# Fused attention and sticky expert routing on one core: own buffers for the DMA-turned exponentials, pair and bias loads issued behind the transpositions, and new keys for the 16-bit products

## The chip, the cores and the metric

One core of one Trainium2 chip runs the whole program. The metric is the device time of one execution in microseconds (us); where several executions are told of, their median stands. The engines are TensorE (PE in the rows; its weight loads, which run beside it, are PEld), VectorE (DVE), ScalarE (ACT), GpSimd (POOL) and SyncE (SP), which here only issues DMAs.

## The reference, cut to what is computed

```
B, H, S, D = 4, 8, 576, 64
scores = q @ k.T / sqrt(D) + bias(|i - j|, i)     # bias: MLP 1 -> 32 -> 8 heads
attn = exp(scores - max);  attn /= attn.sum(-1) + 1e-09
x = (attn @ v), heads side by side                # (4, 576, 512), float32
logits, gate = x @ w_gate, sigmoid(x @ w_local)   # 8 experts
e = argmax(logits[s]) if s == 0 or gate[s] < 0.5 else e of the token before
out[s] = softmax(logits[s])[e] * (relu(x[s] @ w1[e]) @ w2[e])
```

The `bias` depends on the row and the distance only, so it is the same for all four batches. A wrong sign of `gate - 0.5` or a wrong argmax sends a token to another expert, so the scores and the products with the values are computed to about single precision, by pairs of 16-bit numbers (a high half and a low half) where they aren't computed in single precision.

## The kernel before

**Stages.** The bias tables are built first and written to device memory (`bias_d`). Then comes attention, then the routing of the tokens by the logits, then the expert blocks, whose weights stream in from 1 MB loads. The change touches attention alone.

**Pairs and units.** Attention goes through 16 pairs of a batch `b` and two neighbouring heads `p` (`pairs`). A pair has five query tiles in the order 1, 2, 0, 3, 4 (`QORD`), four of 128 rows and one of 64. A unit is one query tile and one head (`hh`); the tile of 64 rows is one unit for both heads, so a pair has 9 units and the program 144. `emit_s(u)` does a unit: TensorE multiplies queries and keys (L305, L306), VectorE adds the bias and takes the row maximum (L325), ScalarE takes the exponential `e` and its row sum (L330).

**Two ways to turn the exponentials.** The products with the values need the exponentials turned, with keys on the partitions. Mostly TensorE turns them (`emit_t`, L398) and ScalarE copies them out (L404). In nine of the pairs, `DMP`, called P0 to P8 here (batch and heads in the order in which the kernel goes through them: heads 1 for four batches, then four pairs of heads 2 and 3, and one more), the first two query tiles, 1 and 2, go another way. ScalarE copies `e` to a 16-bit high half (L336). `emit_lo` has VectorE subtract to get the low half (L346), and SyncE issues one DMA that turns both halves of that query tile at once (L350) into the tile `eT`. The first of the two transpositions of a pair is called T0, the second T1. Then `av_split` does 27 matmuls on 16-bit numbers (L363 and L369) with the pair's values, which `prefetch` splits into 16-bit halves `v16`. The remaining three query tiles go through TensorE and single precision (`emit_av`, L428).

**Buffers.** The turned 16-bit tile takes its place in the pool `et`, two buffers, where the single-precision turned tiles of the other query tiles live too. The pool `e16` for both halves ahead of the transposition has two, `v16` three. A pair's loads land in `qf` (two buffers) and two `kf` (three buffers for both), from which GpSimd casts and subtracts the 16-bit halves `qs`, `kh`, `kl` (four buffers): L122 is such a cast, L119 such a subtraction.

**What goes out.** When a pair is done, `emit_rows` scales its rows, ScalarE makes their 16-bit high halves (L482) and GpSimd the low halves, in the tile `xo` (one buffer). `store_rows` stores them by two DMAs (L492, L495), which for P0 to P8 stand in a list, `stores`, until `LST` units later.

**The order of work.** Steps are put in a list by a key, counted in units: `at(u + 0.1, unit_r, u)` comes 0.1 behind the scores of unit u. `unit_s` emits a unit, `unit_r` what is due of `stores` and `pend` (the query tiles that wait for `emit_lo`). `LA0` holds the keys of the three parts of `av_split`, counted from the last unit of the second query tile. The program is emitted in the order of the keys. From P0 to P8, SyncE runs exactly in that order; the order of the other engines is chosen by a scheduler when the kernel is built, from costs that it assumes.

**Loads.** `prefetch(gi)` is called with the first unit of a query tile. At the first tile of a pair it calls `load_pair` for the pair two further on: four DMAs on SyncE (L141 for `qf`, L143 twice for `kf`, L145 for the values `vt`). At the third tile it loads the next heads' bias tiles (`load_bias`, L166 to L168, three DMAs for one query tile, and L171).

Of the kernel before, what the change touches and what calls it, by code (L numbers as in the profile page):

```python
# [7 lines left out]
F32 = mybir.dt.float32  # L8
F16 = mybir.dt.float16
# [12 lines left out]
NQ = 5  # L22
NP = H // 2
# [5 lines left out]
QORD = (1, 2, 0, 3, 4)  # L29
# [20 lines left out]
def build(tc, nc, io):  # L50
# [20 lines left out]
    def pool(name, bufs, stack=None, **kw):  # L71
        return (stack or p1).enter_context(tc.tile_pool(name=name, bufs=bufs, **kw))
# [4 lines left out]
    et_p = pool("et", 2)  # L77
# [40 lines left out]
    def sub_pool(out, in0, in1):  # L118
        nc.gpsimd.tensor_tensor(out=out, in0=in0, in1=in1, op=ALU.subtract)  # L119
# [134 lines left out]
    pairs = [(p, b) for p in range(NP - 2) for b in range(B)]  # L254
# [7 lines left out]
    e_t, eT_t, hs_t = {}, {}, {}  # L262
    e16_t, v16_t, av_t = {}, {}, {}
    DMP = pairs[B:B + 9]
    dmx = ExitStack()
    dbox = {}
    pend, ucur = [], [0]
    stores, LST = [], 5

    def prefetch(gi):  # L270
        p, b, qt = groups[gi]
        if (p, b) in DMP and qt == QORD[0]:
            if "e" not in dbox:
                open_right()
            v16 = dbox["v"].tile([128, 2, NQ, 128], F16, name="v16")
            nc.vector.tensor_copy(out=v16[:, 0], in_=v_t[b, p])
            sub_pool(v16[:, 1], v_t[b, p], v16[:, 0])
            v16_t[p, b] = v16
        if p == 0:
            if G0 - 6 <= gi < G0 - 1:  # L280
                load_bias(1, QORD[gi - G0 + 6])
            if G0 - 6 <= gi < G0 - 4:
                load_pair(gi - (G0 - 6), 1, wr_t[KORD[-1]])
        else:
            if qt == QORD[0]:
                nx = gi // NQ + 2
                if nx < len(pairs):
                    load_pair(pairs[nx][1], pairs[nx][0])
            if p + 1 < NP and qt == QORD[2]:
                for x in (((0, 1), (2,), (3,), (4,)) if p < NP - 2 else ((0, 1, 2), (3, 4), (), ()))[b]:  # L290
                    load_bias(p + 1, QORD[x])

    def emit_s(u):
        gi, hh = units[u]
        p, b, qt = groups[gi]
        if hh != 1:
            prefetch(gi)
# [45 lines left out]
    def emit_lo(gi):  # L343
        p, b, qt = groups[gi]
        e, e16 = e_t.pop(gi), e16_t.pop(gi)
        nc.vector.tensor_tensor(out=e16[:, 1], in0=e, in1=e16[:, 0], op=ALU.subtract)  # L346
        if (p, b, 0) not in eT_t:
            eT_t[p, b, 0] = et_p.tile([128, 9, 320], F32, name="eT").rearrange("p k i -> p (k i)").bitcast(F16)
        eT = eT_t[p, b, 0][:, 0:18 * 256].rearrange("p (k i) -> p k i", i=256)
        nc.sync.dma_start(  # L350
            out=eT[:, :, QOFF[qt]:QOFF[qt] + 128], in_=e16.rearrange("p t j -> p (t j)"), transpose=True
        )

    def av_split(p, b, part=None):
        if part in (None, 0):
            av_t[p, b, 0] = av_ps.tile([128, 512], F32, name="av")
        av = av_t[p, b, 0]
        eT = eT_t[p, b, 0][:, 0:18 * 256].rearrange("p (t k i) -> p t k i", t=2, i=256)
        v16 = v16_t[p, b]
        terms = ((0, 0), (0, 1), (1, 0))  # L360
        if part in (None, 0):
            for n, (te, tv) in enumerate(terms):
                nc.tensor.matmul(out=av[:, 0:256], lhsT=v16[:, tv, 4], rhs=eT[:, te, 4], start=(n == 0), stop=False)  # L363
        for n, (te, tv) in enumerate(terms):
            if part not in (None, n):
                continue
            for j in range(4):
                for x in range(2):
                    nc.tensor.matmul(  # L369
                        out=av[64 * x:64 * x + 64, 0:256], lhsT=v16[:, tv, j, 64 * x:64 * x + 64],  # L370
                        rhs=eT[:, te, j + 5 * x], start=False, stop=(n == 2 and j == 3),
                    )
        if part not in (None, 2):
            return
        eT_t.pop((p, b, 0))
        v16_t.pop((p, b))
        if (p, b) == DMP[-1]:
            open_w()
        xt = xt_t[p, b] = xt_p.tile([128, SP], F32, name="xt")
        if p >= NP - 2:  # L380
            nc.vector.memset(xt[:, S:SP], 0.0)
        nc.vector.tensor_copy(out=xt[:, 0:256], in_=av[:, 0:256])
# [181 lines left out]
    def open_right():  # L564
        p0.close()
        rbox["x"] = ctx.enter_context(tc.tile_pool(name="x", bufs=2, side="right"))
        rbox["p"] = p2.enter_context(tc.tile_pool(name="rt", bufs=1, side="right"))
        dbox["e"] = dmx.enter_context(tc.tile_pool(name="e16", bufs=2, side="right"))
        dbox["v"] = dmx.enter_context(tc.tile_pool(name="v16", bufs=3, side="right"))
        nc.gpsimd.tensor_copy(out=iota16, in_=iota)  # L570
        nc.gpsimd.tensor_copy(out=ident16, in_=ident)
        nc.gpsimd.tensor_copy(out=amat16, in_=amat[:, 0:2])
# [65 lines left out]
    bias_step(12)  # L638
    LB0, LC0, LO0 = 3.2, 6, 1.28
    LTS = (3.2, 3.2, 2.95, 3.2, 3.95)  # L640
    LA0, LAN, LA1, LL, LOUT = (5.8, 8.55, 8.8), 10.62, (6.35, 6.6), 8.6, 8.72
    NU = len(units)
    ex_t = {}

# [396 lines left out]
            bias_step(BSTEP[s])  # L1041

    def unit_r(s):
        while stores and stores[0][0] <= s:
            store_rows(*stores.pop(0)[1:])
        while pend and pend[0][0] < s:
            emit_lo(pend.pop(0)[1])

    def unit_x(s):
        for st in steps:  # L1050
# [26 lines left out]
    def at(key, f, *a):  # L1077
        ev.append((key, len(ev), partial(f, *a)))

    for u in range(NU):  # L1080
        gi, hh = units[u]
        p, b, qt = groups[gi]
        at(u, unit_s, u)
        at(u + 0.1, unit_r, u)
        at(u + (LB0 if p == 0 else LTS[QORD.index(qt)]), emit_t, u)
        at(u + 0.4, unit_x, u)
        if qt == QORD[1] and hh == 1:
            if (p, b) in DMP:
                for n in range(3):
                    at(u + LA0[n], av_split, p, b, n)  # L1090
            elif p:
                at(u + LAN, emit_av, p, b, 0)
            else:
                at(u + LC0 + 0.6, emit_av, p, b, 0)
        if qt == 4:
            if p:
                if LA1[0] == LA1[1]:
                    at(u + LA1[0], pair_av1, p, b, None)
                else:
                    at(u + LA1[0], pair_av1, p, b, 0)  # L1100
                    at(u + LA1[1], pair_av1, p, b, 1)
                at(u + LL, pair_gates, p, b)
                at(u + LOUT, pair_out, (p, b, gi))
            else:
                at(u + LC0 + 0.6, pair_av1, p, b, None)
                at(u + LC0 + LO0 - 0.01, pair_gates, p, b)
                at(u + LC0 + LO0, pair_out, (p, b, gi))
# [70 lines left out]
    oa, at = rtile([128, NG2, NB], "oa", F16), rtile([128, NG2, NB], "at", F16)  # L1178
# [346 lines left out]
```

## Time and profile before

| | us |
|---|---|
| median of three executions (lowest, highest) | 581.92 (577.92, 582.97) |
| the profiled execution | 580.57 |
| its span, from the first to the last instruction | 578.8 |
| TensorE busy | 529.8 (92%) |
| weight loads of TensorE | 355.9 (61%) |
| VectorE busy | 470.5 (81%) |
| ScalarE busy | 437.1 (76%) |
| GpSimd busy | 263.2 (45%) |

The shares are of the span and are means over all stages. The mean granted TensorE clock was 0.978 of full speed. All durations in the rows below come from the profiled execution, and times of day in them count from the start of its span.

### The profile page before, as it was taken

Reading aid. Unit: us, or ns where it says so; the run is one execution under the profiler, and the core shown is the slowest. Engines: PE = TensorE matmul, PEld = TensorE weight load, DVE = VectorE, ACT = ScalarE, POOL = GpSimd, SP = SyncE. Lnnn points to the kernel's source line nnn. Section 1 sums busy time; section 2 is a strip of 40 time slices with the busy share of each in tenths; the row PEclk is TensorE's granted clock in tenths of the full one; section 3 lists DMA queues with packets and bytes.
Section 4 is the critical chain, followed back from the end, with each engine's and each line's share of the span. In section 5 each row is a group of like instructions: output and inputs, shape, how many; then the busy total and the mean of one; then the engine's idle time right before and its main releaser. Section 6 shows DMA issues by size and latency. Waiting matters only on the chain. (4 is left out here: it accounts for less than half of the span.)

```text
span 578.8 us, 14244 instructions
## 1 busy us (share of the span) xinstructions
PE 529.8 (92%) x5310; PEld 355.9 (61%) x5310; DVE 470.5 (81%) x915; ACT 437.1 (76%) x743; POOL 263.2 (45%) x293
## 2 busy tenths in 40 slices
PE   5669999989979999998999998999999999999992
PEld 1124445766646667766576776587676867777851
DVE  6989885688778898899788458789999799897950
ACT  5879876867878887887589874468998787986940
POOL 5200000894299958967646660522424354344111
PEclk9899999999989999999799999899999999999997
DMA  8766546857798799749174001776899947887250
GB/s 281 259 186 185 144 132 189 267 147 155 192 238 224 190 264 242 198 104 261 33 252 134 22 22 35 257 236 211 271 266 301 333 136 213 160 217 230 18 185 30
DMA packets 104285, 107.33 MB, mean 185 GB/s; under 512 B 71565, under 2 KB 80911, under 8 KB 100114
## 3 DMA queue, kind: packets, MB, share of 16 engines
q1 hardware_dynamic: 99424, 90.63, 56.5%
q0 software_dynamic: 4640, 15.43, 8.8%
q8 instruction: 44, 0.72, 0.5%
q10 hardware_dynamic: 146, 0.30, 0.2%
q14 instruction: 31, 0.25, 0.1%
HBM read 128.92 MB, written 20.80 MB: 259 GB/s over the span
## 5 line engine op out<-in xcount | busy, mean ns | idle before, releaser
L325 DVE CUSTOM_DVE_ANT_0 e<-sps,wb 128x576 f32<-128x576 f32 x144 | 106.8, 747 | 20.0 <-PE sps L306 15.0
L330 ACT ACTIVATE e<-e,st 128x576 f32<-128x576 f32 x144 | 111.5, 775 | 14.2 <-DVE st L325 12.7
L917 DVE TENSOR_TENSOR w<-wb,w 128x2048 bf16<-128x2048 f32 (+1 forms) x36 | 72.3, 2052 | 2.0 <-ACT w L910 2.0
L305 PE MATMUL sps<-kh,qs 128*128 128x288 f16 x256 | 69.5, 293 | 3.3 <-DVE st L325 2.8
L1014 POOL DMA_INDIRECT out_dram<-y,odx x17 | 32.2, 1892 | 88.8 <-ACT y L1004 48.8
L404 ACT COPY eT<-ta 128x512 f32<-128x512 f32 x92 | 52.6, 581 | 23.5 <-PE ta L398 16.6
L398 PE MATMUL ta<-c_cpb,e 128*128 128x128 f32 x432 | 68.1, 278 | 2.0 <-ACT eT L404 1.1
L306 PE MATMUL sps<-kl,qs 128*128 128x288 f16 x256 | 69.2, 291 | 0.0
L988 PE MATMUL yp<-w,hhT 128*128 128x512 bf16 (+1 forms) x272 | 64.9, 381 | 1.1 <-ACT w L910 1.1
L910 ACT CAST w<-wb 128x2048 f16<-128x2048 f32 (+1 forms) x40 | 63.8, 1640 | 2.2 <-DMA wb<-in_w_dram 2.2
L211 PE MATMUL sps<-hd,c_cpa 128*32 128x512 f32 (+17 forms) x352 | 48.3, 505 | 15.1 <-DVE hd L197 10.3
L949 PE MATMUL sps<-xT,we 128*128 128x128 f16 (+1 forms) x1056 | 61.3, 219 | 1.0 <-DVE we L917 1.0
L949 PEld LDWEIGHTS <-we 128*128 128x128 f16 (+1 forms) x1056 | 59.9, 98 | 3.5 <-DVE we L917 1.1
L398 PEld LDWEIGHTS ta<-c_cpb,e 128*128 128x128 f32 x432 | 50.1, 141 | 12.7 <-ACT e L330 2.6
L428 PE MATMUL av<-eT,vt 128*64 128x320 f32 (+1 forms) x368 | 57.7, 425 | 0.0
L197 DVE TENSOR_SCALAR hd<-tab,bp 128x448 f32<-128x448 f32 (+17 forms) x130 | 50.2, 445 | 3.9 <-PE sps L211 3.8
L917 DVE TENSOR_TENSOR we<-ws,we 128x2048 bf16<-128x2048 f32 (+1 forms) x25 | 49.0, 1993 | 2.7 <-ACT we L910 2.6
L949 PEld LDWEIGHTS <-wb 128*128 128x128 f16 (+1 forms) x1056 | 46.9, 98 | 2.8 <-issue 1.5
L949 PE MATMUL sps<-xT,wb 128*128 128x128 f16 (+3 forms) x1056 | 48.5, 207 | 0.0
L988 PEld LDWEIGHTS <-hhT 128*128 128x128 f16 x272 | 25.9, 99 | 30.3 <-issue 2.8
L910 ACT CAST we<-ws 128x2048 f16<-128x2048 f32 (+1 forms) x26 | 41.4, 1637 | 2.1 <-DMA ws<-in_w_dram 2.1
L119 POOL TENSOR_TENSOR qs<-qf,qs 64x288 f16<-64x288 f32 x48 | 40.9, 871 | 1.7
(234 smaller groups left out, 1008.7 us busy)
## 6 DMA issues: line engine op xcount, KB each, us to landing
ws<-in_w_dram SPq DMA_DIRECT2D x34, 1024.0 KB
wb<-in_w_dram SPq DMA_DIRECT2D x34, 1024.0 KB
hs<-in_w_dram SPq DMA_DIRECT2D x20, 1024.0 KB
bias_d<-bv SPq DMA_DIRECT2D x36, 295.5 KB
kf<-in_kt_dram SPq DMA_DIRECT2D x24, 288.0 KB
wb<-bias_d SPq DMA_DIRECT2D x16, 288.0 KB
wb<-bias_d SPq DMA_DIRECT2D x16, 256.0 KB
xrow_d<-xo SPq DMA_DIRECT2D x16, 256.0 KB
```

Of the source, the lines that this page charges most:

```text
L197: nc.vector.tensor_scalar(out=hd[:, 0:n], in0=tab[:, 0:n], scalar1=bp[:, k:k + 1], scalar2=0.0, op0=ALU.add, op1=ALU.max,)
L305: nc.tensor.matmul(out=ps[:, half, 0:288], lhsT=lq, rhs=kh[:, j], start=True, stop=False)
L306: nc.tensor.matmul(out=ps[:, half, 0:288], lhsT=lq, rhs=kl[:, j], start=False, stop=True)
L325: nc.vector.tensor_tensor_reduce(out=e, in0=ps[:, :, 0:288], in1=bsl, scale=-0.125, scalar=1e30, op0=ALU.add, op1=ALU.min, accum_out=st[:, ...
L330: nc.scalar.activation(out=e, in_=e, func=AF.Exp, scale=-1.0, bias=st[:, 0:1], accum_out=sm)
L398: nc.tensor.transpose(out=ta[:, j, :], in_=e[:, o:o + 128], identity=ident)
L404: nc.scalar.copy(out=eTv[:, :, hh, o:o + 128], in_=ta)
L428: nc.tensor.matmul(out=av[64 * x:64 * x + 64, 0:n], lhsT=vt[:, j, 64 * x:64 * x + 64], rhs=eT[:, 2 * j + x, 0:n], start=False, stop=(j == 3),)
L910: nc.scalar.copy(out=wh[c][:, sl], in_=src)
L917: nc.vector.tensor_tensor(out=wl[c][:, sl], in0=src, in1=wh[c][:, sl], op=ALU.subtract)
L949: nc.tensor.matmul(out=hp.rearrange("p a j -> p (a j)")[:, n * f:n * f + n], lhsT=w[f // 4][:, o:o + 128], rhs=x[:, kt], start=(i == 0), s ...
L988: nc.tensor.matmul(out=yp, lhsT=x[:, kt], rhs=w[kt // 4][:, 512 * (kt % 4):512 * (kt % 4) + 512], start=(i == 0), stop=(i == len(terms) - 1),)
```

## The change

It has four parts. The turned 16-bit tile gets a pool of its own, `et16`, with two buffers, and `v16` gets two in place of three. `unit_r` does what is due of `pend` (low half and transposition) ahead of what is due of `stores`, and `LST` goes from 5 to 6. The loads leave `prefetch`: `load_pair` becomes `load_ahead`, with a key 4.15 units into a pair for the first six of P0 to P8 and just ahead of a pair for all others from `p` = 1 on, and the bias loads become `load_next_bias`, 4.2 units into a pair. `LA0` goes from 5.8, 8.55 and 8.8 to 8.2, 9.2 and 9.8.

```diff
@@ emitters
-    stores, LST = [], 5
+    stores = []
     def prefetch(gi):
...
-        else:
-            if qt == QORD[0]:
-                nx = gi // NQ + 2
-                if nx < len(pairs):
-                    load_pair(pairs[nx][1], pairs[nx][0])
-            if p + 1 < NP and qt == QORD[2]:
-                for x in (((0, 1), (2,), (3,), (4,)) if p < NP - 2 else ((0, 1, 2), (3, 4), (), ()))[b]:
-                    load_bias(p + 1, QORD[x])
+
+    def load_ahead(gi):
+        nx = gi // NQ + 2
+        if nx < len(pairs):
+            load_pair(pairs[nx][1], pairs[nx][0])
+
+    def load_next_bias(p, b):
+        if p + 1 < NP:
+            for x in (((0, 1), (2,), (3,), (4,)) if p < NP - 2 else ((0, 1, 2), (3, 4), (), ()))[b]:
+                load_bias(p + 1, QORD[x])
@@ emit_lo
         if (p, b, 0) not in eT_t:
-            eT_t[p, b, 0] = et_p.tile([128, 9, 320], F32, name="eT").rearrange("p k i -> p (k i)").bitcast(F16)
-        eT = eT_t[p, b, 0][:, 0:18 * 256].rearrange("p (k i) -> p k i", i=256)
+            eT_t[p, b, 0] = dbox["t"].tile([128, 18, 256], F16, name="eT16")
+        eT = eT_t[p, b, 0]
@@ open_right
-        dbox["v"] = dmx.enter_context(tc.tile_pool(name="v16", bufs=3, side="right"))
+        dbox["t"] = dmx.enter_context(tc.tile_pool(name="et16", bufs=2, side="right"))
+        dbox["v"] = dmx.enter_context(tc.tile_pool(name="v16", bufs=2, side="right"))
@@ keys
-    LA0, LAN, LA1, LL, LOUT = (5.8, 8.55, 8.8), 10.62, (6.35, 6.6), 8.6, 8.72
+    LA0, LAN, LA1, LL, LOUT = (8.2, 9.2, 9.8), 10.62, (6.35, 6.6), 8.6, 8.72
+    LST, LBI = 6, 4.2
+    LPD, LPN, LPX = 4.15, -0.01, 6
@@ unit_r
+        while pend and pend[0][0] < s:
+            emit_lo(pend.pop(0)[1])
         while stores and stores[0][0] <= s:
             store_rows(*stores.pop(0)[1:])
-        while pend and pend[0][0] < s:
-            emit_lo(pend.pop(0)[1])
@@ the list of steps
         at(u + 0.4, unit_x, u)
+        if p and hh == 0 and qt == QORD[0]:
+            at(u + (LPD if (p, b) in DMP[0:LPX] else LPN), load_ahead, gi)
+            at(u + LBI, load_next_bias, p, b)
```

In the rows of the changed kernel the line numbers are two higher: L352 for a transposition, L307 and L308 for scores, L365 for the first products, L494 and L497 for the stores.

SyncE at P1, before. `eT<-e_1933` is P1's first transposition, `eT<-e_1967` its second, the loads ahead of it are those of P3 and the bias tile of the next heads.

```order
L141 DMA qf<-in_qt_dram 128x576
L143 DMA kf<-in_kt_dram 128x576 x2
L145 DMA vt<-in_vl_dram 128x640
L350 DMA_TRANSPOSE eT<-e_1933 128x18x128
L166 DMA wb_126<-bias_d 128x576
L167 DMA wb_126<-bias_d 128x512
L168 DMA wb_126<-bias_d 128x64
L350 DMA_TRANSPOSE eT<-e_1967 128x18x128
```

SyncE at P1, after.

```order
L352 DMA_TRANSPOSE eT_1938<-e_1901 128x18x128
L352 DMA_TRANSPOSE eT_1938<-e_1935 128x18x128
L141 DMA qf<-in_qt_dram 128x576
L143 DMA kf<-in_kt_dram 128x576 x2
L145 DMA vt<-in_vl_dram 128x640
L166 DMA wb_126<-bias_d 128x576
L167 DMA wb_126<-bias_d 128x512
L168 DMA wb_126<-bias_d 128x64
```

Both transpositions of P1 now stand in a row, ahead of the pair's four loads and the three bias loads.

SyncE after, from P5's second transposition on. The rows L141 to L145 come twice: first P7's loads, behind P5's transpositions and a pair of stores, then P8's. The last two rows are P6's transpositions.

```order
L352 DMA_TRANSPOSE eT_2847<-e_2844 128x18x128
L494 DMA xrow_d<-xo 128x4x128
L497 DMA xrow_d<-xo 64x128
L141 DMA qf<-in_qt_dram 128x576
L143 DMA kf<-in_kt_dram 128x576 x2
L145 DMA vt<-in_vl_dram 128x640
...
L141 DMA qf<-in_qt_dram 128x576
L143 DMA kf<-in_kt_dram 128x576 x2
L145 DMA vt<-in_vl_dram 128x640
L352 DMA_TRANSPOSE eT_3103<-e_3066 128x18x128
L352 DMA_TRANSPOSE eT_3103<-e_3100 128x18x128
```

P8's loads, with the key just ahead of P6, stand between P7's and P6's transpositions; each load into `kf` waits there for a free one of the three buffers.

TensorE at the start of P1's 16-bit products, before. `sps_2232` holds the scores of P2's fifth unit (the four ahead are `sps_2143`, `sps_2160`, `sps_2177` and `sps_2218`).

```order
L305 LDWEIGHTS qs_1643
L305 MATMUL sps_2232<-kh_1644,qs_1643 128x288
L306 LDWEIGHTS qs_1643
L306 MATMUL sps_2232<-kl_1645,qs_1643 128x288
L363 LDWEIGHTS v16_1898
L363 MATMUL av_2105<-eT_1970,v16_1898 128x256
```

TensorE at the same place, after. `sps_2145` holds the scores of P2's third unit (the two ahead are `sps_2111` and `sps_2128`).

```order
L307 LDWEIGHTS qs_1726
L307 MATMUL sps_2145<-kh_1727,qs_1726 128x288
L308 LDWEIGHTS qs_1726
L308 MATMUL sps_2145<-kl_1728,qs_1726 128x288
L365 LDWEIGHTS v16_1889
L365 MATMUL av_2159<-eT16_1938,v16_1889 128x256
```

P1's products stand behind three units of P2 where they stood behind five.

## Rows read from the trace of the kernel before

**Rows 1.** Stretches: from and to, us, busy of each engine, PEclk, DMA share, GB/s.

```profile
127.10:277.20 150.10, 138.87 (x1185) 95.91 (x1185) 128.92 (x333) 119.77 (x276) 112.59 (x128) 0.98 0.81 202
168.00:172.00 4.00, 4.00 (x25) 2.21 (x21) 2.28 (x5) 2.42 (x7) 3.78 (x6) 0.57 0.58 138
272.00:284.00 12.00, 10.37 (x69) 5.66 (x70) 9.88 (x27) 4.64 (x10) 11.70 (x17) 0.72 0.36 116
```

**Rows 2.** Waits of TensorE, 127 to 278: who for what, us, times, longest.

```profile
PE av L363 <- DMA eT<-e: 6.0, 3, 3.4
```

**Rows 3.** Timeline of TensorE: start, us, engine, instruction, idle before and its releaser.

```profile
147.39 0.49 PE L363 MATMUL av<-eT,v 128*128 128x256 f16 x3 [1.39 <-DMA eT<-e]
...
166.76 0.49 PE L363 MATMUL av<-eT,v 128*128 128x256 f16 x3 [3.35 <-DMA eT<-e]
...
272.67 0.50 PE L363 MATMUL av<-eT,v 128*128 128x256 f16 x3 [1.21 <-DMA eT<-e]
```

**Rows 4.** Timeline of SyncE, its issues of DMAs.

```profile
140.43 4.83 SPq L350 DMA_TRANSPOSE eT<-e  x1
...
159.88 3.27 SPq L350 DMA_TRANSPOSE eT<-e  x1
163.19 0.58 SPq L141 DMA_DIRECT2D qf<-in_qt_dram  x1
...
169.07 1.79 SPq L350 DMA_TRANSPOSE eT<-e  x1
...
226.60 0.58 SPq L141 DMA_DIRECT2D qf<-in_qt_dram  x1
...
267.82 1.99 SPq L350 DMA_TRANSPOSE eT<-e  x1
```

**Rows 5.** Timeline of VectorE: low halves (L346) and a pair's first scores (L325).

```profile
135.32 1.35 DVE L346 TENSOR_TENSOR e<-e,e 128x1152 f16<-128x1152 f32 x1
...
154.82 1.35 DVE L346 TENSOR_TENSOR e<-e,e 128x1152 f16<-128x1152 f32 x1
...
159.75 0.75 DVE L325 CUSTOM_DVE_ANT_0 e<-sps,wb 128x576 f32<-128x576 f32 x1
...
164.28 1.52 DVE L346 TENSOR_TENSOR e<-e,e 128x1152 f16<-128x1152 f32 x1
...
178.09 0.75 DVE L325 CUSTOM_DVE_ANT_0 e<-sps,wb 128x576 f32<-128x576 f32 x1
...
187.00 1.36 DVE L346 TENSOR_TENSOR e<-e,e 128x1152 f16<-128x1152 f32 x1
...
241.24 0.75 DVE L325 CUSTOM_DVE_ANT_0 e<-sps,wb 128x576 f32<-128x576 f32 x1
...
258.01 0.74 DVE L325 CUSTOM_DVE_ANT_0 e<-sps,wb 128x576 f32<-128x576 f32 x1
...
265.15 1.35 DVE L346 TENSOR_TENSOR e<-e,e 128x1152 f16<-128x1152 f32 x1
```

**Rows 6.** Timeline of GpSimd: casts (L122), key and row low halves (L119).

```profile
164.55 2.51 POOL L119 TENSOR_TENSOR xo<-xr,xo 128x640 bf16<-128x640 f32 x1
...
167.46 1.41 POOL L122 TENSOR_SCALAR qs<-qf 64x576 f16<-64x576 f32 x2 [0.41 <-DMA qf<-in_qt_dram]
...
174.44 2.80 POOL L119 TENSOR_TENSOR kl<-kf,kh 128x288 f16<-128x288 f32 x4
...
181.31 1.41 POOL L122 TENSOR_SCALAR qs<-qf 64x576 f16<-64x576 f32 x2
...
189.49 2.82 POOL L119 TENSOR_TENSOR kl<-kf,kh 128x288 f16<-128x288 f32 x4
...
193.65 1.40 POOL L119 TENSOR_TENSOR xo<-xr,xo 128x640 bf16<-128x640 f32 x1
...
230.32 2.40 POOL L122 TENSOR_SCALAR qs<-qf 64x576 f16<-64x576 f32 x2 [1.69 <-DMA qf<-in_qt_dram]
```

**Rows 7.** Timeline of ScalarE: the 16-bit high half of P0's rows.

```profile
159.35 0.71 ACT L482 CAST xo<-xr 128x640 f16<-128x640 f32 x1
```

More of the change, by code (lines that the diff above doesn't have):

```diff
@@ L357, in av_split @@
         av = av_t[p, b, 0]
-        eT = eT_t[p, b, 0][:, 0:18 * 256].rearrange("p (t k i) -> p t k i", t=2, i=256)
+        eT = eT_t[p, b, 0].rearrange("p (t k) i -> p t k i", t=2)
         v16 = v16_t[p, b]
```

## The prediction

> **What bounds the kernel now.** I read the busy times by stage first, then who waits for whom, then the three instructions that wait. The nine pairs whose exponentials are turned by DMA (P0 to P8, batch and head pairs in the order of the kernel) fill 127.1 to 277.2 us. In these 150.1 us TensorE is busy for 138.9 and VectorE for 128.9, ScalarE for 119.8, GpSimd for 112.6 [rows 1]: TensorE is the bound, with 11.2 us of gaps. Of its waits one kind stands out: L363, the first of the 16-bit products, waits 6.0 us in three places for a DMA transposition [rows 2]. They are 1.39 us at P0's products, 3.35 at P1's and 1.21 at P8's [rows 3].
>
> What follows two of them costs as much again. TensorE stood still from 163.41 to 166.76, and from 168 to 172 the granted clock has a mean of 0.57, that is stretches at the lower of its two levels (1.2 in place of 2.4 GHz). Around P8's wait, from 272 to 284, the mean is 0.72. After P0's 1.39 us it did not fall. Work that a full clock would have done is 4.0 x 0.43 = 1.7 us and 12.0 x 0.28 = 3.4 us [rows 1].
>
> Why the transpositions come late is seen in SyncE's rows. A transposition with nothing ahead of it is issued in 1.79 us; P0's second took 4.83, behind six bias loads; P1's second 3.27, behind three [rows 4]. From the end of the issue to the end of TensorE's wait it is 2.1 us (145.26 to 147.39), 3.6 (163.15 to 166.76, the next pair's loads issued right behind it from 163.19) and 2.9 (269.81 to 272.67) [rows 3, 4]. The data had been ready: VectorE's low halves (L346) of the second tile ended at 136.67 for P0 and 156.17 for P1, the issues began at 140.43 and 159.88 [rows 4, 5].
>
> **The change part by part.**
> *Transpositions ahead of loads.* P0's second can start at 136.7, with an issue of some 1.8 to 2.9 us and 2.1 to 3.6 to land: by 143.2 at the latest, where TensorE comes at 146.0. That wait goes: 1.39. P1 moves up by 1.4: low halves ready at 154.8, landed at 158.7 to 161.3. In the order of instructions P1's products now stand behind three score units of P2, before behind five. TensorE came there at 163.41; less 1.4 and two units of about 1 us each (a guess from the spacing of its scores) it is 160. I take this wait as gone (3.35), with little to spare. At P8 the store pair between low halves and transposition goes: start at 266.50 and not 267.82, 1.3 us against a wait of 1.21, gone by a hair. Sum of waits 6.0; with the clock after P1 and P8, 1.7 + 3.4, **11.1 us** at most, where the clock's part is the less sure one.
>
> *Own buffers.* Before, the turned tile shares two buffers with the single-precision one, so a first transposition waits for products on TensorE: P2's began at 169.07, though its low halves were done at 165.80 [rows 4, 5]. That wait goes and is behind the 11.1 already, since nothing waited for it on TensorE. Two 16-bit value tiles in place of three: the next write comes two pairs later, behind products that are done by then; nothing.
>
> *Products further back.* The planner puts them behind three units at P1, P4 and P5 (before five), one unit later at P0, four later at P6 (five units into P7). It is the same work: 0.
>
> *Loads behind transpositions, stores and their queue.* This costs, since it takes 10 to 13 us off the lead of the pair loads. The load of a pair two ahead now follows T0, T1 and the store of rows of two pairs back; that store waits for GpSimd's rows (xo), which stand behind GpSimd's casts of the load before. So there is a ring: casts, xo, store, load, casts. Its length: casts of seven pairs last 9.8 us (167.46 to 177.24) to 11.0 (181.31 to 192.31), I take 10.5, in the middle; xo 1.40; two stores 1.1 (P8's transposition at 267.82 stands 1.3 behind the low halves for them, 0.2 of it waking); load to first cast 3.72 (226.60 to 230.32) to 4.27 (163.19 to 167.46), I take 3.7, where the queue ahead was clear. Sum **16.7** [rows 4 to 6], against pairs of 15.98 on average (178.09 to 258.01, five) [rows 5]. With TensorE 6.5 us earlier from P3 on (1.4, 3.35, 1.7):
> - P3 starts at 171.6. Its casts start behind P0's xo, whose ScalarE cast was at 159.35 [rows 7], now about 158.7, so at 161.2 at the latest, and end by 171.7; the first head's are done 1.4 earlier, and TensorE starts some 1.2 before the first score is read. Cost 0 to 0.8, taken 0.4.
> - P4's load follows P2's second transposition. In P3 today the low halves end 10.3 us into the pair (188.36 less 178.09); P2 then starts at 158.4, so 168.7, plus 2.0 for the issue, 1.1 for the store, 3.7: casts from 175.6 to 186.1. Three rounds of 16.7 on, P7's end at 236.2, its first head at 234.8. P7 starts at 234.7 (241.24 less 6.5), TensorE needs it at 233.5. Cost 1.3.
> - P8's load stands right behind P7's, ahead of P6's transpositions, and its second key tile needs a buffer that P7's first head frees at 234.8. So T0 and T1 of P6 are issued from 235.6 to 239.2 and land at 241 to 242. The products wait for neither (five units into P7), but ScalarE, which writes P7's halves into the same two tiles, waits to about 239.5: 0 to 2, taken 0.8.
> - P8's casts follow at 239.0, first head done at 248.1 (9.1 in), then the rest of P9's load, and P7's transpositions from 248.9 to 252.5, landed at 254.6 to 255.4. P8 starts at 252.8 (258.01 less 6.5 plus 1.3) and the products follow its first unit, at 253.0 to 253.8. Cost 0.8 to 2.4, taken 1.6.
> Sum 4.1. **Net 11.1 - 4.1 = 7.0 us.**
>
> The profiled execution took 580.57 us, 1.8 more than its span, and lies 1.35 below the median of 581.92. So 573.6 for an execution like it, 574.9 for the median. What follows P8 (scores in single precision, routing, expert blocks) keeps its order and its bound, so I let the gain pass through to the end.
>
> **The rivals.**
> *The ring becomes the bound (slower).* With the high ends, 11.0 + 1.40 + 1.1 + 4.27 and 1.40 for a value tile that comes in line, a round takes 19.2 us. From P3 to P7 that is 4 x (19.2 - 16.0) = 12.8 lost, and with 4.0 for late transpositions and a clock that falls again (3.4): 20.2 - 11.1 = +9, or 591. It turns slower from about 17.8 a round on ((11.1 - 4.0) / 4 above 16.0). For it: GpSimd was busy for 3.78 of 4 us at 168 to 172 [rows 1], and its xo took 2.51 us at 164.55, while VectorE's two-input L346 ran from 164.28 to 165.80, against 1.40 at 193.65 [rows 5, 6]. Against it: the 10.5 already holds what VectorE cost in seven pairs.
> The Trainium skill, page "SBUF — State Buffer", section "Who interferes with whom", says that a VectorE instruction with two SBUF inputs and a GpSimd instruction that reads SBUF exclude each other for the whole instruction; the 1.11 us that xo took longer agree. By that rule, two L346 a pair that each hold GpSimd up by this much would put the ring at 18.9 and the time with this rival; by the mean of the casts they are in the sum.
>
> *Waits go, the rest is taken back (within 1%).* P1's and P8's transpositions land a little later than I think, or the clock falls at P8 for its small routing products and not for the wait: 6.0 - 4.1 = 1.9, or 580.0. For it: P8's margin is 0.1 us, P1's is within its spread, and the products were meant further back but in the planner's order stand earlier at P1, so that the change does not do there what it says.
>
> *Nothing is taken back.* 11.1 off: 570.8. It needs GpSimd's rounds at 16.0 (9.8 + 1.40 + 1.1 + 3.72) in every pair.
>
> **How the numbers follow.** A measurement tells about 1% (5.8 us) from no change: the three runs of before lie 5.05 apart. Forecast (5.8 to 10 us off, at 574.9) 0.42; nothing taken back 0.10; within 1% 0.37; the ring 0.11. Faster is the first two, 0.52. The range goes from 569, the full gain with some of the runs' spread, to 584, the second rival with the same; it leaves out most of the ring and little else.
>
> **What would show it.** Right: no wait of L363 for a DMA at P0, P1 and P8; clock 1.00 in the stretch after P1's products; transposition issues near 2 us; P0 to P8 in some 143 us. GpSimd's rows should show xo, store, load and casts in a ring of 16 to 17 us, SyncE should stand before the second key tile of P8's load for some 8 us, and P7's products should wait 1 to 2 us. Wrong: score products waiting for GpSimd's casts from P5 on by several us each, VectorE's value casts waiting for loads, or a clock of 0.5 around 272 that stays without any wait ahead of it.

## The result, and the profile after

| | before | after |
|---|---|---|
| median of 14 executions (lowest, highest), us | 581.85 (575.96, 583.86) | 586.61 (583.18, 588.76) |
| ratio to before, 95% interval | | 1.0097 (1.0073 to 1.012) |
| profiled execution, us | 580.57 | 585.61 |
| its span, us, and mean granted clock | 578.8, 0.978 | 583.8, 0.983 |
| P0 to P3, P3 to P7, P7 to the end of P8, us | 51.0, 63.2, 35.9 | 46.4, 68.4, 40.2 |

The change made the kernel slower by 0.97%, 4.8 us by the medians, where 7.0 less were forecast and the range ended at 584. The profiled executions lie 5.04 apart and stand for the medians. The last line of the table divides the nine pairs by their first scores on VectorE: 127.10, 178.09 and 241.24 before, with 277.16 as the end, and 127.65, 174.00, 242.39 and 262.65 plus 19.97 after. So 4.6 us were gained by the start of P3, 5.2 were lost in the four pairs from there, and 4.3 in P7 and P8. What follows P8 took as long as before.

Stretches after: the nine pairs, the time behind P1's products, P4, P8, and the routing behind P8 (to [rows 1]).

```profile
127.65:282.62 154.97, 138.56 (x1182) 96.09 (x1182) 130.23 (x334) 120.34 (x274) 113.42 (x127) 0.99 0.72 194
162.00:167.00 5.00, 4.62 (x47) 3.07 (x46) 3.57 (x8) 4.97 (x11) 3.42 (x4) 1.00 0.95 331
190.90:209.15 18.25, 17.23 (x138) 11.05 (x138) 14.33 (x38) 13.12 (x30) 13.54 (x14) 0.91 0.66 170
262.65:282.60 19.95, 16.19 (x132) 10.71 (x132) 19.30 (x58) 13.62 (x32) 13.77 (x18) 1.00 0.53 137
279.00:291.00 12.00, 10.22 (x82) 5.87 (x83) 11.51 (x31) 6.79 (x16) 6.98 (x11) 1.00 0.45 129
```

TensorE has the same 138.6 us of work in a stretch 4.9 longer. The clock behind P1's products and behind P8 is full, as forecast, and yet P8 takes 19.95 us: VectorE is busy for 19.30 of them.

TensorE after: who it waited for (total, times, longest), and its timeline (to [rows 2, 3]). L416 turns a query tile's last key columns into `tb_r`.

```profile
PE tb_r L416 <- DVE xr L475: 3.7, 2, 2.3
...
PE av L365 <- DMA eT<-e: 3.1, 2, 2.2
...
146.93 0.49 PE L365 MATMUL av<-eT,v 128*128 128x256 f16 x3
161.58 0.50 PE L365 MATMUL av<-eT,v 128*128 128x256 f16 x3
190.13 0.33 PE L416 MATMUL tb_r<-c_cpb,e 128*128 128x128 f32 x1 [2.27 <-DVE xr L475]
241.65 0.33 PE L416 MATMUL tb_r<-c_cpb,e 128*128 128x128 f32 x1 [1.46 <-DVE xr L475]
247.86 0.50 PE L365 MATMUL av<-eT,v 128*128 128x256 f16 x3 [2.25 <-DMA eT<-e]
279.30 0.50 PE L365 MATMUL av<-eT,v 128*128 128x256 f16 x3 [0.87 <-DMA eT<-e]
```

The waits at P0's and P1's products are gone. In their place TensorE waits for VectorE's `xr`, the scaled rows of the pair before (L475 reads them out of `tb_r`, the tile that L416 writes next), and P6's products wait 2.25 for their transposition. No wait names GpSimd's casts, where the forecast put the cost.

VectorE after: its wait for GpSimd in P0 to P8, and the rows L470 (first part of `xr`) and two first scores (to [rows 5]).

```profile
DVE xr L470 <- POOL xo L119: 7.8, 4, 2.6
...
174.00 0.75 DVE L327 CUSTOM_DVE_ANT_0 e<-sps,wb 128x576 f32<-128x576 f32 x1
189.20 0.69 DVE L470 TENSOR_TENSOR xr<-ta,sums 128x512 f32<-128x512 f32 x1 [2.57 <-POOL xo L119]
206.29 0.69 DVE L470 TENSOR_TENSOR xr<-ta,sums 128x512 f32<-128x512 f32 x1 [1.19 <-POOL xo L119]
223.39 0.69 DVE L470 TENSOR_TENSOR xr<-ta,sums 128x512 f32<-128x512 f32 x1 [1.62 <-POOL xo L119]
240.51 0.69 DVE L470 TENSOR_TENSOR xr<-ta,sums 128x512 f32<-128x512 f32 x1 [2.46 <-POOL xo L119]
242.39 0.74 DVE L327 CUSTOM_DVE_ANT_0 e<-sps,wb 128x576 f32<-128x576 f32 x1
```

`xr` has one buffer. VectorE can't write a pair's rows before GpSimd has subtracted the rows of the pair before into `xo`. No such wait is in the trace of before.

GpSimd after: casts of a load, and `xo` (to [rows 6]).

```profile
176.89 1.41 POOL L122 TENSOR_SCALAR qs<-qf 64x576 f16<-64x576 f32 x2 [1.20 <-DMA qf<-in_qt_dram]
187.77 1.39 POOL L119 TENSOR_TENSOR xo<-xr,xo 128x640 bf16<-128x640 f32 x1
193.78 1.42 POOL L122 TENSOR_SCALAR qs<-qf 64x576 f16<-64x576 f32 x2 [3.26 <-DMA qf<-in_qt_dram]
204.86 1.40 POOL L119 TENSOR_TENSOR xo<-xr,xo 128x640 bf16<-128x640 f32 x1
221.96 1.40 POOL L119 TENSOR_TENSOR xo<-xr,xo 128x640 bf16<-128x640 f32 x1
239.07 1.41 POOL L119 TENSOR_TENSOR xo<-xr,xo 128x640 bf16<-128x640 f32 x1
```

SyncE after: stores, the loads behind them, and the load and the transposition at the start of P6 (to [rows 4]).

```profile
189.19 0.38 SPq L494 DMA_DIRECT2D xrow_d<-xo  x1
...
190.18 0.58 SPq L141 DMA_DIRECT2D qf<-in_qt_dram  x1
...
206.29 0.39 SPq L494 DMA_DIRECT2D xrow_d<-xo  x1
...
229.66 8.42 SPq L143 DMA_DIRECT2D kf<-in_kt_dram  x2
...
238.66 3.36 SPq L352 DMA_TRANSPOSE eT<-e  x1
```

This is the ring of the prediction, read off directly: casts from 176.89, `xo` from 187.77 to 189.16, store from 189.19, load at 190.18, the next casts at 193.78. The `xo` follow each other by 17.09, 17.10 and 17.11 us, and the four pairs from 174.00 to 242.39 take 17.1 on average (16.9, 18.3, 16.1, 17.1), against 15.8 before. VectorE's L470 goes off within 0.05 us of the end of each `xo`. Then the two key tiles of P8's load take 8.42 us to issue, where those of other loads take 0.9: SyncE stands before the second, and P6's transpositions, queued behind, start at 238.66.

### The profile page after: what moved, and what is told of

It reads as the page before. It is cut to its first block, busy times and chain, and to the rows that moved or that the text cites. A ratio compares the mean times of both kernels' runs of the same rounds, so it can differ in the third digit from the quotient of the medians.

```text
span 583.8 us, 14236 instructions
## 1 busy us (share of the span) xinstructions
PE 528.8 (91%) x5310; PEld 356.0 (61%) x5310; DVE 473.3 (81%) x915; ACT 438.4 (75%) x743; POOL 264.6 (45%) x293
## 5 line engine op out<-in xcount | busy, mean ns | idle before, releaser
L332 ACT ACTIVATE e<-e,st 128x576 f32<-128x576 f32 x144 | 111.9, 778 | 19.1 <-DVE st L327 16.3
L327 DVE CUSTOM_DVE_ANT_0 e<-sps,wb 128x576 f32<-128x576 f32 x144 | 106.5, 746 | 15.3 <-PE sps L308 10.8
L307 PE MATMUL sps<-kh,qs 128*128 128x288 f16 x256 | 68.9, 291 | 4.1 <-DVE st L327 3.4
L308 PE MATMUL sps<-kl,qs 128*128 128x288 f16 x256 | 68.3, 288 | 0.0
L1019 POOL DMA_INDIRECT out_dram<-y,odx x17 | 29.4, 1731 | 83.2 <-ACT y L1009 45.4
L211 PE MATMUL sps<-hd,c_cpa 128*32 128x512 f32 (+17 forms) x352 | 49.8, 538 | 15.5 <-DVE hd L197 10.1
L954 PE MATMUL sps<-xT,we 128*128 128x128 f16 (+1 forms) x1056 | 61.1, 219 | 0.0
L400 PEld LDWEIGHTS ta<-c_cpb,e 128*128 128x128 f32 x432 | 50.4, 142 | 11.1 <-ACT e L332 2.9
L954 PE MATMUL sps<-xT,wb 128*128 128x128 f16 (+3 forms) x1056 | 48.5, 207 | 0.0
L119 POOL TENSOR_TENSOR qs<-qf,qs 64x288 f16<-64x288 f32 x48 | 41.6, 885 | 1.7
```

The source lines that it names most:

```text
L307: nc.tensor.matmul(out=ps[:, half, 0:288], lhsT=lq, rhs=kh[:, j], start=True, stop=False)
L308: nc.tensor.matmul(out=ps[:, half, 0:288], lhsT=lq, rhs=kl[:, j], start=False, stop=True)
L327: nc.vector.tensor_tensor_reduce(out=e, in0=ps[:, :, 0:288], in1=bsl, scale=-0.125, scalar=1e30, op0=ALU.add, op1=ALU.min, accum_out=st[:, ...
L332: nc.scalar.activation(out=e, in_=e, func=AF.Exp, scale=-1.0, bias=st[:, 0:1], accum_out=sm)
L400: nc.tensor.transpose(out=ta[:, j, :], in_=e[:, o:o + 128], identity=ident)
L954: nc.tensor.matmul(out=hp.rearrange("p a j -> p (a j)")[:, n * f:n * f + n], lhsT=w[f // 4][:, o:o + 128], rhs=x[:, kt], start=(i == 0), s ...
```

## The experiments

Each ratio is to the kernel before in runs beside it, with its 95% interval. The last three columns are, as above, from the profiled execution, in us.

| run | ratio to before | P0 to P3 | P3 to P7 | P7, P8 |
|---|---|---|---|---|
| e1 store behind load | 0.9997 (0.9968 to 1.0027) | 46.6 | 67.5 | 38.5 |
| e2 loads first | 0.9897 (0.9865 to 0.9928) | 49.5 | 61.1 | 35.8 |
| e3 all loads late | 1.0056 (1.0021 to 1.009) | 46.4 | 68.2 | 36.2 |
| e4 xo on VectorE | 1.0074 (1.0032 to 1.0115) | 49.4 | 62.8 | 40.1 |
| e5 own buffers alone | 0.9982 (0.9951 to 1.0013) | 51.1 | 64.6 | 35.9 |
| e6 order alone | 0.9994 (0.9956 to 1.0033) | 48.5 | 63.7 | 36.1 |
| e7 loads first, old keys | 0.9934 (0.9906 to 0.9963) | 48.7 | 61.6 | 36.3 |
| e8 store behind load, all late | 1.0009 (0.9973 to 1.0045) | 46.5 | 66.4 | 35.3 |
| e9 loads between transpositions | 1.0025 (0.9978 to 1.0071) | 46.2 | 66.0 | 40.0 |
| e10 order, store late | 0.9963 (0.9922 to 1.0004) | 49.1 | 65.1 | 37.4 |
| e11 xo on VectorE, all late | 0.9953 (0.9912 to 0.9994) | 51.2 | 61.8 | 33.2 |
| e12 two loads late | 1.0 (0.9961 to 1.004) | 46.7 | 68.8 | 34.7 |
| e13 loads first, xo on VectorE | 0.9918 (0.9878 to 0.9957) | 46.7 | 62.1 | 34.3 |
| e14 xo on VectorE, all late, store behind | 1.0043 (1.0012 to 1.0074) | 46.8 | 67.4 | 35.1 |

A profiled execution can lie off the median of its run: e1's took 584.18 against 580.6, e2's 579.69 against 575.24, e8's 583.39 against 580.37. So the ratios decide, and the stretches say where to look. A changed key also moves instructions on the other engines, since their order is chosen anew at each build.

**Store behind the load** (the changed kernel with):

```diff
-    LST, LBI = 6, 4.2
+    LST, LBI = 7, 4.2
```

> The changed kernel with LST 7 in place of 6, which puts the store of a pair's rows behind the next pair loads on SyncE. Theory A (ring): the changed kernel lost its gain because store, load, casts and xo form a ring of 17.1 us that sets the pace from P3 to P7 (68.4 us for four pairs, 63.2 before). With the load no longer behind the store the ring is cut: P3 to P7 take 63 to 66, VectorE waits for GpSimd's xo under 3 us in place of 7.8, and the time falls to 579 to 583. Theory B (GpSimd is late because the loads stand behind the transpositions, whatever the stores do): P3 to P7 stay at 67 to 69 and the time at 585 to 587.

The time was theory A's: 580.6 us, 1.0% below the changed kernel, with the intervals well apart. The mechanism was not what A named: in the profiled execution VectorE waited 6.5 us for `xo`, and P3 to P7 took 67.5, where A had 63 to 66. The store's place costs; how, this run leaves open.

**Loads first:**

```diff
-    LPD, LPN, LPX = 4.15, -0.01, 6
+    LPD, LPN, LPX = 4.15, -0.01, 0
```

> The changed kernel with LPX 0, so that every pair load is issued just ahead of a pair, as the kernel before did; transpositions still stand ahead of stores and bias loads. Theory A and B both: the loads leave the ring and come 10 us earlier, P3 to P7 take 63 to 65, the 8.4 us that SyncE stood before the second key tile of P8's load go, and the gain of the first three pairs (4.1 at P3) stays: 575 to 579. Theory C (the extra pool and the products' keys cost by themselves, through the order of the other engines): 582 to 586.

575.24 us, 1.0% faster than before and 2% faster than the change as made. That is the largest effect of one number, and it settles the question of which part lost the time: all other parts of the change are in this kernel, and it wins. VectorE's wait for `xo` is not in its trace. Its first scores of P3 and P7:

```profile
179.13 0.75 DVE L327 CUSTOM_DVE_ANT_0 e<-sps,wb 128x576 f32<-128x576 f32 x1
...
240.25 0.75 DVE L327 CUSTOM_DVE_ANT_0 e<-sps,wb 128x576 f32<-128x576 f32 x1
```

61.1 us for four pairs, where the change took 68.4 and the kernel before 63.2.

**All loads late:**

```diff
-    LPD, LPN, LPX = 4.15, -0.01, 6
+    LPD, LPN, LPX = 4.15, -0.01, 9
```

> The changed kernel with LPX 9, so that the loads of the last three pairs of the nine also come behind the transpositions. Theory A: the 8.4 us stand of SyncE before the second key tile goes and P6's transpositions are issued some 7 us earlier, but the ring of 17.1 goes on through P8: P7 falls from 20.3 to 17 to 18.5, P3 to P7 stay at 68, the time comes to 582 to 585. Theory D (the stand of SyncE is the main cause): P7 falls to 16.8 and the time to 580 to 581.

584.22 us and 68.2 from P3 to P7, as theory A had it; D fell. SyncE's stand is gone (P8's two key tiles are issued in 0.9 us and not in 8.42), P7 takes 17.6 in place of 20.3 and P8 18.6 in place of 20.0. The pair behind P8 took 21.0 in place of 19.1, so half of that came back at once, and the intervals of the two ratios overlap. `xo` still comes every 16.9 us (187.58 to 255.20, four rounds).

**xo on VectorE** (the changed kernel with):

```diff
-        (sub_dve if on_act and (p, b) != (NP - 1, B - 2) else sub_pool)(lo, xr, hi)
+        (sub_dve if (on_act and (p, b) != (NP - 1, B - 2)) or (p, b) in DMP else sub_pool)(lo, xr, hi)
```

> The changed kernel with the low halves of the nine pairs' rows on VectorE in place of GpSimd, so that neither the store nor VectorE's next rows wait for GpSimd. It adds some 0.75 us a pair to VectorE (6.8 in all) by the rate of its low halves (1.35 us for 1152). Theory A: the ring is cut on the other side, P3 to P7 take 64 to 66, the time falls to 580 to 584. Theory B: P3 to P7 stay at 68 or more with the added work on VectorE: 586 to 590.

582.82 us, as A said, with P3 to P7 below A's 64 to 66. First scores of P3 and P7, and TensorE at P6's products:

```profile
177.01 0.74 DVE L327 CUSTOM_DVE_ANT_0 e<-sps,wb 128x576 f32<-128x576 f32 x1
...
239.76 0.75 DVE L327 CUSTOM_DVE_ANT_0 e<-sps,wb 128x576 f32<-128x576 f32 x1
...
247.31 0.82 PE L365 MATMUL av<-eT,v 128*128 128x256 f16 x3 [4.08 <-DMA eT<-e]
```

With the loads as late as ever, four pairs take 62.8 us once `xo` is off GpSimd. So what held TensorE in this stretch was not the casts but the `xo` that stood behind them. SyncE's stand remained (7.58 us for the two key tiles) and cost 4.08 at P6's products.

**Own buffers alone, order alone, and both with the loads first.** e5 is the kernel before with

```diff
-            eT_t[p, b, 0] = et_p.tile([128, 9, 320], F32, name="eT").rearrange("p k i -> p (k i)").bitcast(F16)
+            eT_t[p, b, 0] = dbox["t"].tile([128, 18, 256], F16, name="eT16")
...
-        dbox["v"] = dmx.enter_context(tc.tile_pool(name="v16", bufs=3, side="right"))
+        dbox["t"] = dmx.enter_context(tc.tile_pool(name="et16", bufs=2, side="right"))
+        dbox["v"] = dmx.enter_context(tc.tile_pool(name="v16", bufs=2, side="right"))
```

> The kernel before with the own pool for the turned 16-bit tiles (and two v16) as the only change; loads, bias loads, stores and keys as before. Theory A (the gain of the change comes from the order on SyncE): the second transpositions of P0 and P1 still stand behind bias loads, TensorE's waits for them stay at 4 to 6 us, no change beyond 0.5% (579 to 584 by the median before). Theory E (a shared buffer was what held the transpositions up): the waits fall under 2 us and the time by 4 to 8 us.

No change, and TensorE's waits for transpositions are the old ones: 5.5 us.

e6 is the kernel before with the two loops of `unit_r` exchanged and the bias loads taken out of `prefetch`:

```diff
+        while pend and pend[0][0] < s:
+            emit_lo(pend.pop(0)[1])
         while stores and stores[0][0] <= s:
             store_rows(*stores.pop(0)[1:])
-        while pend and pend[0][0] < s:
-            emit_lo(pend.pop(0)[1])
...
+        if p and hh == 0 and qt == QORD[0]:
+            at(u + 4.2, load_next_bias, p, b)
```

> The kernel before with the order on SyncE as the only change: low half and transposition ahead of stores, and bias loads behind the second transposition; pair loads, buffers, LST and keys as before. Theory A: TensorE's waits at P0 and P1 go (4.7 of 6.0 us) with the fallen clock behind P1, 4 to 7 us off: 575 to 578. Theory E: without buffers of their own the first transpositions wait for TensorE and these waits come back: 580 to 582.

580.21 us, no change by the ratio: the time is in theory E's range, but A was right on P0, whose wait is gone. The waits for transpositions were 4.1 us in three places (0.89 at P1, 1.18 at P2, 2.07 at P8), and P0 to P3 took 48.5 against 51.0; at the whole time nothing of it shows (the profiled execution, 3.5 us above the run's median, came to P0 3.1 us later than that of before). e7 is e2 with the first line below, e10 is e6 with the second:

```diff
+    LA0, LAN, LA1, LL, LOUT = (5.8, 8.55, 8.8), 10.62, (6.35, 6.6), 8.6, 8.72
...
-    stores, LST = [], 5
+    stores, LST = [], 6
```

> The run with the loads first (LPX 0, 575.2 us) with the keys of the products as before (5.8, 8.55, 8.8). Theory A (the keys cost and give nothing, TensorE does the same work in any of these places): within 2 us of it, 573 to 577. Theory F (the new keys give the transpositions the time that they need): waits of TensorE for transpositions of 3 us or more, 578 to 581.

> The run with the order on SyncE alone (580.2 us), with LST 6 in place of 5, so that stores come behind the second transposition: the run with the loads first and old keys (576.2 us) but with shared buffers. Theory G (own buffers are worth nothing alone but some 4 us once the order is changed): 579.5 to 581. Theory H (what the order alone lacked was the store behind the second transposition): 576 to 577.5.

576.15 us, as theory A had it, and 579.12, between theories G and H. From e6 over e10 and e7 to e2 the ratios fall from 0.9994 over 0.9963 and 0.9934 to 0.9897. The ends are apart; each single step is inside the intervals. So store place, own buffers and keys together give about 1% on top of the order, and which of them gives how much stays open. That the new keys give nothing, as I had costed them, is not refuted.

**Store behind the load, all loads late** (e1 and e3 together):

```diff
-    LST, LBI = 6, 4.2
-    LPD, LPN, LPX = 4.15, -0.01, 6
+    LST, LBI = 7, 4.2
+    LPD, LPN, LPX = 4.15, -0.01, 9
```

> The changed kernel with LST 7 and LPX 9: stores behind the pair loads, and the loads of all nine pairs behind the transpositions, so that neither the ring through the store nor the stand of SyncE before P8's second key tile is left, only the late loads. Theory A (the ring through the store is what costs): P3 to P7 in 62 to 65 us, 575 to 579, as with the loads first. Theory B (loads that come late put GpSimd's xo behind the casts of the load, and VectorE, with one buffer of rows, behind xo, ring or not): VectorE still waits 5 us or more for xo, P3 to P7 take 66 to 68, 579 to 583.

Theory B: 66.4 us from P3 to P7, VectorE's waits for `xo` 5.1 us, 580.37 us. Without the store in it there is no ring any more: `xo` comes at 188.41, 203.73, 218.42, 237.31 and 249.61, 15.3 apart on average. But each is late by the casts ahead of it, and VectorE waits. P3 to P7 are 1.8 us shorter than in e3, and 1.5 of that lie in P4, whose clock did not fall here. P4 in e3, then in e8 (columns as in [rows 1]):

```profile
190.69:208.98 18.29, 17.26 (x139) 11.12 (x138) 14.36 (x39) 13.11 (x30) 13.41 (x14) 0.91 0.66 169
191.51:208.32 16.81, 15.56 (x142) 10.36 (x141) 14.23 (x39) 12.99 (x30) 14.87 (x17) 1.00 0.77 208
```

**xo on VectorE, all loads late** (the diffs of e4 and e3 together):

> The run with the rows' low halves on VectorE (582.8 us) with LPX 9 as well, so that SyncE does not stand before P8's second key tile. Theory: the two losses of the changed kernel lie in different stretches and add up, xo behind casts in P3 to P7 (62 to 64 us here, 68.4 in the changed kernel) and SyncE's stand in P7 and P8 (35.5 to 37 us here, 40.2 in the changed kernel): 577.5 to 580.5. If the late casts hold TensorE by themselves, whoever makes xo: P3 to P7 66 or more, 582 to 585.

577.59 us, P3 to P7 in 61.8, P7 and P8 in 33.2: both losses are gone, though every load is still behind the transpositions. From e4 to e11 (SyncE's stand) the ratio falls from 1.0074 to 0.9953, from e3 to e11 (`xo`) from 1.0056; both pairs of intervals are apart. P0 to P3 took 51.2 here, 4.8 more than in the change: P2 took 18.81, and the clock stood at its lower level behind a wait of 1.61 for VectorE's `st`. TensorE at that wait, and the stretch behind it:

```profile
169.55 0.28 PE L307 MATMUL sps<-kh,qs 128*128 128x288 f16 x1 [1.61 <-DVE st L327]
...
172.00:178.00 6.00, 5.59 (x30) 4.74 (x31) 3.96 (x13) 2.56 (x7) 2.60 (x3) 0.50 0.92 213
```

**Two loads late** (e12, the first added line) and **loads between the transpositions** (e9, the second):

```diff
-    LPD, LPN, LPX = 4.15, -0.01, 6
+    LPD, LPN, LPX = 4.15, -0.01, 2
...
+    LPD, LPN, LPX = 2.15, -0.01, 9
```

> The changed kernel with LPX 2: the loads that P0 and P1 issue behind the transpositions, all others just ahead of a pair. Theory: the late loads cost nothing before the ring has closed, and the first three pairs were shorter with them (46.3 us against 49.5 with all loads first), so P0 to P3 46 to 48, P3 to P7 61 to 63, P7 and P8 36: 572 to 575. If the ring, once begun, goes on: P3 to P7 65 or more, 577 to 580.

> The changed kernel with LPD 2.15 and LPX 9: the loads of all nine pairs between the first and the second transposition, ahead of the store. Theory B, as the runs so far have shaped it (what costs is how late the load is: behind the store most, behind the second transposition half of that, because GpSimd's xo comes behind the casts and VectorE's rows behind xo): P3 to P7 between the 61.1 of the loads first and the 66.4 of loads late with stores behind them, 62 to 65; VectorE waits under 3 us for xo; 575 to 578.5. Theory A (the store ahead of the load alone): no ring, so as with the loads first, P3 to P7 61 to 62, 573.5 to 575.5.

Both missed. In e12 the ring did not go on, but the change from late to early loads put a stand of SyncE into P2, before the second key tile of P4's load. SyncE, then TensorE at P2's products:

```profile
165.05 0.38 SPq L143 DMA_DIRECT2D kf<-in_kt_dram  x1
174.50 0.33 SPq L143 DMA_DIRECT2D kf<-in_kt_dram  x1
...
175.40 6.35 SPq L352 DMA_TRANSPOSE eT<-e  x2
...
183.35 0.82 PE L365 MATMUL av<-eT,v 128*128 128x256 f16 x3 [6.32 <-DMA eT<-e]
```

From 165.43 to 174.50 nothing is issued, both transpositions wait behind, and P2's products stand 6.32 us; P3 took 22.4 us at a mean clock of 0.85. It is the same stand as the changed kernel's at P6, at a place where the products follow fewer units behind.

In e9, at 581.96 us, VectorE did not wait for `xo`. The second transpositions are slow again behind the loads, P2's by the row of SyncE, and P2's products wait:

```profile
168.18 4.48 SPq L352 DMA_TRANSPOSE eT<-e  x1
...
175.63 0.71 PE L365 MATMUL av<-eT,v 128*128 128x256 f16 x3 [2.22 <-DMA eT<-e]
```

That is part of it; what holds P8 there for 22.6 us I did not find.

**Loads first with xo on VectorE** (e13, the diffs of e2 and e4 together), and **xo on VectorE, all loads late, store behind** (e14, those of e4 and e8):

> The run with the loads first (575.2 us) with the rows' low halves on VectorE as well, which takes 1.4 us a pair from GpSimd and gives some 0.75 to VectorE. Theory I (with xo off GpSimd late loads are free, and what the run with late loads and xo on VectorE, 577.6, lacks to the loads first is VectorE's added work): 576.5 to 579 here, no faster than with the loads late. Theory J (late loads cost some 2 us of their own, whatever xo does): 573 to 575.5 here.

> The run with late loads and xo on VectorE (577.6 us) with LST 7, so that the stores stand behind the loads. Theory I (the store ahead of the load costs only because it waits for GpSimd's xo): within 1.5 us of 577.6, where the same step of LST with xo on GpSimd took 3.8 off (584.2 to 580.4). Theory K (the store ahead of the load costs by its place on SyncE, whoever makes xo): 573 to 575.

e13, at 575.5 us, is at the edge of theory J; its interval overlaps e11's, so whether late loads cost some 2 us by themselves stays open. e14, at 583.53, missed both theories, by 4 us on the far side. With `xo` on VectorE nothing waits for GpSimd's, and yet P3 to P7 took 67.4, with a row of small waits of TensorE for VectorE (`xt` 3.1 us, `sums` 4.1). So a late `xo` is not the only thing that can make this stretch long. From e11 to e14 the store's move costs 0.9%, from the change to e1 it gives 1.0%; as the other engines' order is chosen anew with it, I have no cause for the difference.

## Why the prediction was wrong

**The waits that go: right in place, too large in sum.** P0's and P1's waits went, the clock stayed up behind P1, SyncE stood before P8's second key tile, 8.42 us for the two, where a stand of some 8 was forecast. By the start of P3 the gain is 4.6 us, of 6.5 forecast: P1's stretch shrank by 0.4 and not 1.39 (a wait of 0.80 for VectorE's `xt` took its place at 152.31), P2's by 4.3 of 5.05. The 4.6 forecast at P8 (1.21 and the clock's 3.4) came not at all: the wait went from 1.21 to 0.87, and at a full clock P8 still took 19.95 us, for VectorE fills it. VectorE was busy for 17.2 us in P8 before. The 2.1 more are small instructions, mostly of the routing, more of them and longer ones; why is open. The clock's share there was costed as if TensorE bounded that stretch; in [rows 1] VectorE's 9.88 of 12 us beside TensorE's 10.37 at a clock of 0.72 should have warned me.

**Where the 12 us lie.** The forecast was 7.0 less, and the profiled executions say 5.0 more. Ahead of P3 the miss is 1.9 us (4.6 gained of 6.5), from P3 to P7 it is 3.5 (5.2 lost, not 1.7), in P7 and P8 it is 6.5 (4.3 lost where 2.2 were to be gained). The step named next made the second miss; the largest, the third, comes below it and in the 4.6 above that did not come at P8.

**The step that failed: "TensorE needs it at 233.5. Cost 1.3".** The ring was found, and its length was nearly right: 16.7 forecast, 17.1 measured (casts 10.8 to 11.1, `xo` 1.4, stores 1.0, load to cast 3.6 to 3.9). But I charged it only at one exit, the casts that the scores need, where a lead of some microseconds lets three rounds pass before anything is late. TensorE never waited there. There is a second exit with no lead: `xo` frees the one buffer of `xr`, VectorE's rows wait for it, and behind VectorE's rows stand TensorE's turns. So P3 to P7 lost 4 x (17.1 - 15.8) = 5.2 us in place of 1.7 (0.4 and 1.3). P3 to P7 before, then after (columns as in [rows 1]):

```profile
178.09:241.24 63.15, 59.88 (x525) 41.65 (x523) 54.54 (x138) 51.81 (x119) 53.77 (x60) 1.00 0.89 223
174.00:242.39 68.39, 61.16 (x526) 42.96 (x525) 53.18 (x137) 52.99 (x119) 56.32 (x61) 0.98 0.77 214
```

TensorE is idle for 7.2 us in place of 3.3, and 3.7 of the 7.2 are the two waits for `xr`, 2.27 and 1.46. It is also busy for 1.3 more, at a clock that fell in P4, behind the first of these waits. e4 and e11, which take `xo` off GpSimd and leave the loads late, agree: 62.8 and 61.8 us from P3 to P7.

What is not shown is that the ring has to close for this. In e1 and e8 the store is behind the load, so that no ring is left, and P3 to P7 still took 67.5 and 66.4, with VectorE waiting 6.5 and 5.1 us for `xo`. A load so late that its casts stand ahead of `xo` is enough.

The one buffer was in the code, and that VectorE writes `xr` and GpSimd reads it too. I had followed the ring's casts to their readers, not `xo` to its writer.

**The second loss: P7 and P8.** I had SyncE's stand and the late transpositions of P6 behind it, put them at 235.6 to 239.2, and let the products "wait for neither". The casts ended 3 us later than I had them, the first transposition began at 238.66, and the products waited 2.25. e3, without SyncE's stand, took 36.2 in place of 40.2. P7's products, where I had 1.6, did not wait: all that is left of waits for transpositions is the 2.25 at P6's and the 0.87 at P8's. P7 and P8 lost 4.3 us, where by my terms (0.8 and 1.6 lost, 4.6 gained) they should have gained 2.2.

**The rival that came nearest** is the first one, the ring becomes the bound: right in sign and in P3 to P7, though a closed ring is not shown to be the cause. I priced its round at 19.2 and its turning point at 17.8. With the gain really there (4.6, not 11.1) the turning point is nearer to the old pace: with the 4.3 lost in P7 and P8, any round above 15.9 (4.6 less 4.3 over four pairs, above 15.8) ends slower. So 11% was too little for it, mainly because the gain against which it was weighed had been taken whole. (The 4.0 for late transpositions in it is worked out nowhere; the high ends of the two bullets on them give 4.4.) The 18.9 us for a round counted twice what the casts already hold, as that passage's last clause suspected. In each of the four rounds two of GpSimd's single casts or subtractions of 0.67 to 0.73 us took 1.75 to 1.86, each beside an L348 of VectorE, and these some 2.2 us are part of the casts' 10.8 to 11.1. Four subtractions beside an L348, four with none, and that L348:

```profile
183.91 3.90 POOL L119 TENSOR_TENSOR kl<-kf,kh 128x288 f16<-128x288 f32 x4
...
236.31 2.81 POOL L119 TENSOR_TENSOR kl<-kf,kh 128x288 f16<-128x288 f32 x4
...
183.52 1.62 DVE L348 TENSOR_TENSOR e<-e,e 128x1152 f16<-128x1152 f32 x1
```

So the trace agrees with the rule of the Trainium skill that I weighed there (page "SBUF — State Buffer", section "Who interferes with whom"), and the round is still 17.1. `xo` itself met no L348 in these rounds (1.40 each time); in e8 one did, at 249.61, and took 2.52 us.

**Own buffers at nothing:** right for the buffers alone (e5). **Products' keys at nothing:** within the intervals (e7 against e2).

What is settled: the late loads turn a change that else wins 1% into one that loses 1% (e2), and with `xo` on VectorE and no stand of SyncE they need not (e11). What is not: how much of the loss is the store ahead of the load. Moving it gave 1.0% in e1 against the change, and in e8 against e3 0.5%, whose intervals overlap; their traces still show VectorE waiting for `xo`, and e14 goes the other way.

## What to carry to other kernels

When a transfer is moved back in a queue, follow it around until it meets itself: load, casts, whatever stands behind the casts on that engine, the store that waits for it, the next load. If it closes, compare its length with the pace of the loop. Closed or not, ask of every instruction that the late transfer pushes back who waits for it, and charge the delay at the exit with the least lead. Here that was a single-buffered tile and not the data that was moved.

A load that waits for a buffer holds up everything behind it on its queue: changing from late to early loads (P6 in the change, P2 in e12) makes such a stand even where both orders by themselves have none.

## What the runs showed of the hardware

A transposition with nothing issued just ahead of it was issued in 1.78 to 2.00 us (e9's first ones); right behind a pair's four loads the second ones took 3.52 to 4.49 us. Both turn tiles of the same shape; what differs is what was issued ahead of them.

The granted clock fell to the lower level behind single waits of TensorE as short as 1.21 us (P8 before, 0.72 over the 12 us of [rows 1]), 1.61 (e11) and 2.27 (P3 after, then 0.91 over P4). It stayed at 1.00 behind the 1.39 at P0's products before and the 2.25 at P6's products after. The length of the wait alone does not tell it.
